# One-core sparse attention and mixture of experts: a new hand-written order of all steps, a rotated identity for the key turns, split loads of the first batch, merged weight loads, and a reciprocal written back to PSUM

## The chip, the cores and the metric

One Trainium2 chip, one of its cores, one launch. The time is device microseconds (us) of that core. The engines named below are TensorE (PE; PEld is its weight load), VectorE (DVE), ScalarE (ACT), GpSimd (POOL) and SyncE (SP, which here only issues transfers). POOL issues transfers too; they are called software transfers here, after the profile's name for their queue.

## The reference

Two stages on batch 4, 8 heads, 768 positions, head size 64. The first is a sparse attention: each query sees its neighbours nearer than 16 positions and 24 summaries (one for each block of 32 keys: the largest key value of each column, and the mean of the block's values). The second takes the result, 768 x 512 for each batch, through a router and four causal attention experts of head size 64, of which each position uses the best two.

```python
k_sum = k.reshape(B, H, nb, block, D).max(axis=3)      # nb = 24, block = 32
v_sum = v.reshape(B, H, nb, block, D).mean(axis=3)
scores_l_m = np.where(abs(i - j) < 16, scale * q @ k.T, -1e9)
scores_s = scale * q @ k_sum.T + log(block)
attn = softmax(concat(scores_l_m, scores_s)) @ concat(v, v_sum)
x = attn  # heads side by side: (B, 768, 512)
logits = x @ w_gate                                     # 4 experts, the best 2 with their weights w
for e in range(4):
    a = softmax(causal(scale * (x @ wq[e]) @ (x @ wk[e]).T))
    out += w_e * (a @ (x @ wv[e]) @ wo[e])
```

## The kernel before

The program is a plan of named steps, each a few instructions on one engine, and a table written out by hand (`TABLE`) that lists every step once, in one global order, with the engine that does it (P, V, A, G or S for PE, DVE, ACT, POOL, SP) and the buffer or PSUM bank that each new tile takes. Each engine runs its own steps strictly in the order of the table; waits between engines follow from who writes and reads which part of which tile. PSUM has eight banks and every tile class a fixed number of slots (`SLOTS`), so the table also fixes who waits for a slot.

Names are step, batch, then a number. For the first stage a batch has four pairs of heads (0 to 3), and two groups of two pairs, which share a load of keys and queries:

- Loads: `dk`, `dq` (keys, queries of a group, software transfers with a cast to 16 bits, issued by POOL), `dv` (values of a pair, four transfers from SP), `dvs` (values once more in the layout for block means, four transfers).
- `hc` copies the 32-row edges of the value tile `vb`, on POOL, ACT or DVE. Block means: `bs` (PE with the constant `sel`), `be` (DVE, four instructions) and `ds` (spreads the means into rows 96 to 119 of `vb`), or for the groups in `TREE` adds on POOL (`tr`, L340, the first of 1,024 columns and then 512 to 64) and `ds`.
- `tk`, `tq` (PE turns keys and queries, L359), `kw` (keys out of PSUM into windows), `rk` (block maximum, DVE), `ksc` (the maxima copied beside each window), `cq` (queries out of PSUM), `sc` (scores: the mask `mt` times `pi`, L407, then L413), `ex` (exponentials on ACT, L420), `av` (times `vb`, L430), `rc` and `xm` (normalising, DVE), `tx` (turn, L455), `hi`, `lo` (two 16-bit halves).
- Second stage, per batch: `vp` (values and router logits, L539 and L542), `lg`, `v2` (copies), `ga`, `gx`, `gb`, `gc` (router), and for two pairs of experts `pp`, `pc` (queries and keys, L607), six blocks of `sp`, `es`, `dm` (scores L631, exponentials L639, causal mask on POOL L644), `aw` (times values, L655), `r2` (reciprocal L674, times the router's weight L676), `wv` (L681), `tw`, `ct` (turn and copy), and per batch `op`, `oc`, `od` (output matmul L709, copy, store).

`r2` takes the column of sums (column 64 of each block) out of PSUM: L674 writes its reciprocal to the small SBUF tile `cmb`, and L676 multiplies `cmb` by the router's weight `gt`, both in SBUF, back into `cmb`.

The key tiles `kn` are 100 rows: two rows of zeros, 96 of keys, two of zeros. Setup fills each of the three whole (`knz`, L219, DVE), so a key load waits for that fill. The turn with the plain identity puts the zero columns at both ends of each 100.

A step `fill` exists that runs matmuls on zeros; the table before doesn't use it. The first instructions before are, on POOL, `dk001 dk000 dq001 id16 dq000 mt sel hc00`, where `id16`, `mt` and `sel` make constants.

Of the kernel before, what the change touches and what calls it, by code (L numbers as in the profile page):

```python
# [15 lines left out]
S = 768  # L16
# [44 lines left out]
227,P,3.1.0 246,V, 14,G, 53,P,6.0.0 54,A, 34,S,3 229,V, 96,P,0.1 97,A, 70,P,4.1.1 35,G, 36,P,2.1 55,V, 207,G,2
231,P,0.1 217,G,0 114,S,0 115,S, 216,G,0 71,A, 247,A, 37,V, 33,G, 38,V, 118,S, 84,P,6.0.2 72,V, 230,G, 83,P, 85,V,
232,A, 248,P,2.2 228,A, 86,V, 249,A, 100,P,0.1.0 101,P, 117,S, 102,V, 103,V, 235,P,4.3 250,P,2.2 87,P,6.2.2 236,A,
251,A, 88,V, 89,V, 252,P,4.4 122,G, 104,P,0.3.3 261,P,2.2.2 253,A, 105,A, 106,V, 278,P,3.0.0 280,V, 124,G, 265,P,4.0
282,P,5.2 262,A, 279,A, 283,A, 263,V, 281,V, 266,A, 210,S,4 208,S,5 209,G, 168,P,0.0 170,P,6.1 264,G, 233,P,2.5 234,A,
169,V, 211,G, 212,P,0.0 284,P,2.1 116,S,1 267,P,4.0 113,S, 171,V, 110,S, 119,S, 121,V, 129,P,6.0.0 285,A, 213,V,
215,A, 109,S, 112,S, 214,V, 268,A, 131,V, 130,A, 126,P,0 127,V, 132,P,2 134,A, 108,S, 111,S, 123,V, 222,S,0 128,V,
178,P,4.0 133,V, 135,V,0 175,P,6 176,A, 376,G,1 184,P,0 185,A, 223,G, 238,P,2.0.1 237,P, 239,V, 240,V, 255,P,6.1.2
179,A, 254,P, 256,V, 257,V, 136,A, 137,V, 224,G,0 180,G, 187,P,0 269,P,2.3 188,A, 189,G, 186,G, 241,P,4.4.4 242,V,
243,V, 218,S,0 120,S, 270,A, 172,P,0 173,A, 181,P,6 182,A, 139,P,2.2 140,A, 258,P,0.5.5 259,V, 260,V, 177,G, 183,G,  # L70
138,V, 141,P,6.0 174,G, 191,P,0.0.2 192,P, 219,A, 220,S,1 190,P, 193,V, 194,V, 286,P,0.5 221,V, 142,A, 158,P,4.0
225,G, 272,P,6.0.0 381,S,0 287,A, 159,A, 146,P,0 147,A, 152,P,4 153,A, 375,G,1 149,P,2 271,P, 273,V, 274,V, 150,A,
226,G, 288,P,0.1.1 289,P, 155,P,4 143,P,6 156,A, 386,G,2 275,P,2.6.6 290,V, 291,V, 144,A, 276,V, 277,V, 292,P,0.7.7
382,G, 293,A, 294,V, 195,P,4.0 125,A, 151,G, 401,P,5.1 196,A, 402,V, 383,G,1 397,P,6.1.1 160,G, 154,G, 399,V,
418,P,7.0 419,A, 339,P,2.1 340,A, 398,V, 337,P,0.0 148,G, 145,G, 162,P,1.1.4 161,P, 157,G, 163,P, 164,V, 165,V,
379,S,2 338,A, 356,P,0.1 341,P,2 385,V, 298,P,6.1.1 300,V, 299,V, 342,A, 357,A, 400,A, 344,P,4 384,G,3 380,G, 345,A,
353,P,2 354,A, 295,P,0 296,V, 297,V, 301,P,6 302,A, 350,P,0 351,A, 403,P,2.4 377,S, 358,G, 347,P,4 303,V, 414,P,6.2.0
551,S,0 304,V,1 416,V, 348,A, 404,A, 431,P,7.0.2 433,V, 390,S,5 308,P,0.2 309,A, 166,P,4.1 167,A, 310,P,2.0 311,A,
405,P,0.2 406,A, 417,V, 432,V, 305,A, 200,P,4.0 415,V, 546,G,2 312,P,2.0 327,P,6 328,A, 556,G,0 422,P,0.3 378,G,
387,G,0 346,G, 355,G, 420,P,6.0 201,V, 306,V, 307,V, 349,G, 313,A, 352,G, 421,A, 343,G, 360,P,0.0.4 423,A, 361,P,  # L80
359,P, 362,V, 363,V, 203,P,2.1 204,A, 435,P,6.2 436,V, 324,P,0 325,A, 545,G,1 315,P,4 316,A, 364,P,7.2 552,G, 553,G,0
365,V, 197,P,2.2 555,G,4 321,P,0 322,A, 448,P,6.1.1 329,G, 198,V, 450,V, 451,V, 318,P,4 434,G, 452,P,7.1 453,V,
425,P,2.0.2 319,A, 567,P,0.2.0 569,V, 424,P, 426,V, 427,V, 408,P,4.1.0 449,A, 456,P,6.1 391,G, 407,P, 409,V, 410,V,
568,A, 457,A, 570,V, 437,P,0.5 438,A, 392,S,0 454,P,2.3 455,A, 317,G, 571,P,6.0 588,P,7.1 584,P,0.1.2 585,A, 572,A,
205,S, 326,G, 557,G,1 589,V, 320,G, 323,G, 314,G, 586,V, 330,P,1.1.4 331,P, 332,P, 333,V, 334,V, 439,P,2.0 411,P,0.0.0
440,A, 393,G, 394,G,1 396,V, 388,S,0 573,P,6.2 574,A, 587,A, 395,G, 575,P,2.4 576,A, 412,V, 428,P,4.1.1 413,V, 389,G,
199,S, 458,P,6.1.1 459,P, 429,A, 590,P,2.3 442,P,0.0.2 460,V, 461,V, 591,A, 430,V, 441,P, 605,P,2.2 443,V, 444,V,
592,P,6.1 606,A, 335,P,3.3 462,P,4.2.2 463,V, 445,P,0.3.3 464,V, 336,A, 369,P,2.1 593,A, 446,A, 447,V, 562,S,0 563,G,
564,G,1 366,P,6.2 367,A, 507,P,4.1 509,P,0.0 508,V, 370,A, 202,S, 565,V,1 468,P,2.0.0 469,V, 510,A, 526,P,0.1 520,P,4
554,G,2 527,A, 528,G, 547,S, 470,V, 521,A, 522,G, 465,P,6 466,A, 467,V, 511,P,0 514,P,2 512,A, 622,P,4.0 623,V,  # L90
618,P,5.0.1 515,A, 620,V, 471,P,6 516,G, 523,P,0 473,A, 472,V, 517,P,2 621,G, 524,A, 601,P,4.2.0 518,A, 525,G, 619,V,
372,P,6.0 373,A, 603,V, 478,P,0.2 479,A, 602,V, 558,S, 474,V,0 480,P,2.0 481,V, 548,G, 578,P,4.1.0 475,A, 513,G,
577,P, 476,V, 477,V, 371,S, 497,P,0.0 498,A, 549,S, 604,G, 607,P,2.0 626,P,6.5 579,V, 580,V, 519,G, 529,P,0.0.0 368,S,
531,P, 608,A, 530,P, 627,A, 532,V, 533,V, 624,P,2.4 625,A, 491,P,6 492,A, 550,G, 595,P,4.0.1 374,S, 499,G, 594,P,
596,V, 597,V, 609,P,0.2 610,A, 485,P,2 581,P,6.4.4 582,V, 488,P,4 486,A, 566,G,3 583,V, 489,A, 559,G, 612,P,0.1.2
611,P, 560,S, 561,G, 613,V, 614,V, 598,P,2.5.5 599,A, 482,P,4 628,P,6.0.0 483,A, 629,P, 600,V, 494,P,0 630,V, 493,G,
487,G, 631,V, 495,A, 615,P,2.6.6 616,A, 617,V, 534,P,4.0 535,V, 632,P,6.7.7 490,G, 484,G, 496,G, 502,P,1.1.0 501,P,
500,P, 503,V, 504,V, 633,A, 648,P,2.1 649,A, 650,P,4.0 651,A, 634,V, 505,P,0.1 681,P,2.2 682,V, 661,P,4.1 658,P,6
506,A, 536,P,0.1 537,V, 638,P,2.1.1 640,V, 662,A, 659,A, 664,P,4 665,A, 667,P,6 639,A, 641,P,0 642,V, 668,A, 655,P,4
656,A, 666,G, 657,G, 652,P,2 653,A, 643,A, 683,P,6.0 538,S, 684,V, 635,P,4 636,V, 660,G, 669,G, 644,V,1 700,P,0.0  # L100
701,A, 663,G, 654,G, 688,P,2 689,A, 690,G, 637,V, 539,P,6.2 540,V, 541,S, 685,P,0 702,G, 671,P,0.0.4 645,A, 686,A,
670,P, 694,P,2 695,A, 672,P, 646,V, 647,V, 677,V, 678,V, 687,G, 696,G, 673,V, 691,P,0 697,P,6 674,V, 542,P,2.0 692,A,
693,G, 704,P,1.1.0 703,P, 706,V, 707,V, 698,A, 699,G, 675,P,4.2 543,A, 544,S, 705,P, 710,V, 711,V, 676,A, 679,P,2
680,A, 708,P,3.3 712,P,2 713,V, 720,P,2.1 709,V, 721,A, 722,S, 714,P,0.2 715,V, 716,S, 717,P,4.0 718,A, 723,P,0.1
719,S, 724,A, 725,S,
# [51 lines left out]
def make_plan(nc, T, q, k, v, moe_w_gate, moe_wq, moe_wk, moe_wv, moe_wo, out):  # L157
# [23 lines left out]
    vones, knzs = [st("vo0"), st("vo1")], [st("kz0"), st("kz1")]  # L181
# [24 lines left out]
    def vone(i0, i1):  # L206
        def go(e):
            for t in T["vb"][i0:i1]:
                en(e).memset(t[0:96, :, 64:65], 1.0 / XS)
                en(e).memset(t[96:128, :, 64:65], 32.0 / XS)  # L210
                en(e).memset(t[0:16, 0:24:12, :], 0.0)
                en(e).memset(t[64:96, 11:24:12, :], 0.0)  # L212
                en(e).memset(t[64:80, 11:24:12, 64:65], 1.0 / XS)
        return go

    def knz(i0, i1):
        def go(e):
            for t in T["kn"][i0:i1]:
                en(e).memset(t, 0.0)  # L219
        return go  # L220
# [27 lines left out]
    def load_qk(b, g, parts):  # L248
        n = 4 // parts
        kn[b, g], qn[b, g] = R.buf("kn"), R.buf("qn")  # L250
        for i in range(parts):
            h0 = 4 * g + n * i

            def gk(e, t=kn[b, g], i=i, h0=h0):
                nc.gpsimd.dma_start(
                    out=T["kn"][t.slot][PE0:PE0 + 96, n * i:n * i + n, :],
                    in_=k[b, h0:h0 + n].rearrange("h (p s) d -> p h (s d)", s=8))

            def gq(e, t=qn[b, g], i=i, h0=h0):
                nc.gpsimd.dma_start(  # L260
                    out=T["qn"][t.slot][:, n * i:n * i + n, :],
                    in_=q[b, h0:h0 + n].rearrange("h (p s) d -> p h (s d)", s=QT))
            R.step(f"dk{b}{g}{i}", {"G": 0.72}, knzs[0:1] if (b, g) == (0, 0) else knzs, [kn[b, g]], gk, dma=n * 96 * 0.098 / 16)
            R.step(f"dq{b}{g}{i}", {"G": 0.72}, [], [qn[b, g]], gq, dma=n * 128 * 0.077 / 16)

    vb, vr = {}, {}
# [594 lines left out]
```

## Time and profile before

| | us |
|---|---|
| median of 3 runs | 185.4 |
| the three runs | 181.22, 185.4, 187.53 |
| the profiled execution | 181.54 |
| its span, first to last instruction | 179.6 |
| outside the span (the difference) | 1.94 |

The profile is one execution. Busy time of an engine is the sum of its instructions; the slices cut the span into 40 parts of 4.49 us and show the busy share of each in tenths. The chain of work is followed back from the last instruction, at each step to what released it. An idle time is given in brackets with what ended it. In section 6 of the page the last number is the time from a transfer's issue to its landing. The chain has 50% of the span on PE, 30% on DVE, 7% on "issue", 4% each on ACT and transfers and 2% on POOL.

### The profile page before, as it was taken

The numbers are of one execution on the slowest core, as the hardware profiler recorded it, in microseconds if no ns is written. First come the engines' busy times: TensorE is split into PE (matmuls) and PEld (weight loads), VectorE is DVE, ScalarE is ACT, GpSimd is POOL, SyncE is SP. The second block draws the span as 40 slices with busy tenths as digits, with TensorE's granted clock in tenths as the row PEclk, the third lists the DMA queues.
The fourth block names the chain that finished last, engine by engine and source line by source line (L and its number), as shares of the span: only waits on it lengthen the run. The fifth ranks groups of instructions, "written<-read, shape, count | busy, mean of one in ns | idle before, by whom it ended". The sixth has DMA issues, their size and how long they took to land.

```text
span 179.6 us, 6545 instructions
## 1 busy us (share of the span) xinstructions
PE 147.4 (82%) x2784; PEld 110.7 (62%) x2784; DVE 135.9 (76%) x265; ACT 120.1 (67%) x155; POOL 99.3 (55%) x150
## 2 busy tenths in 40 slices
PE   0247569899999999979969959899988899999660
PEld 0235558677679778657546858766757787565420
DVE  5763875999796989897998929866999878538640
ACT  2056667947688978876987837476947674789640
POOL 5866353440993599987986990861377520053100
PEclk9999999999999999999999969999999999999996
DMA  4999999989985996499939959806461000032326
GB/s 72 167 217 229 217 161 192 213 166 169 220 143 122 151 168 96 113 145 200 161 84 217 251 128 210 178 4 184 141 169 39 7 0 4 0 120 105 127 98 257
DMA packets 44221, 25.34 MB, mean 141 GB/s; under 512 B 33216, under 2 KB 40384, under 8 KB 43712
## 3 DMA queue, kind: packets, MB, share of 16 engines
q1 hardware_dynamic: 36736, 18.63, 47.5%
q0 software_dynamic: 7456, 6.29, 23.6%
q8 instruction: 22, 0.36, 0.8%
q14 instruction: 7, 0.06, 0.1%
HBM read 24.91 MB, written 6.29 MB: 174 GB/s over the span
## 4 chain that ended last, share of the span: by engine, by line
PE 50%; DVE 30%; issue 7%; ACT 4%; DMA 4%; POOL 2%; DVEq 0%; ACTq 0%; POOLq 0%
PE ps L430 10%; PE ps L607 7%; PE ps L455 5%; PE ps L359 4%; PE ps L539 4%; PE ps L709 4%; DMA qn<-in_q_dram 4%; DVE vb L168 3%; PE ps L655 3%; DVE ks L375 3%; PE ps L631 3%; PE ps L407 3%; PE ps L297 3%; DVE wav L681 3%; DVE cmb L676 2%
## 5 line engine op out<-in xcount | busy, mean ns | idle before, releaser
L639 ACT ACTIVATE a<-ps 128x1024 f16<-128x1024 f32 (+1 forms) x48 | 41.9, 916 | 9.8 <-PE ps L631 8.8
L644 POOL TENSOR_SCALAR_AFFINE_SELECT a<-a 128x256 f16<-128x256 f16 x48 | 18.7, 408 | 37.7 <-ACT a L639 26.7
L420 ACT ACTIVATE aT<-ps 120x768 f32<-120x768 f32 x32 | 25.3, 817 | 10.0 <-PE ps L413 7.5
L340 POOL TENSOR_TENSOR vt<-vt 120x1024 f32<-120x1024 f32 (+3 forms) x20 | 25.1, 1254 | 5.7 <-DMA vt<-in_v_dram 4.5
L430 PE MATMUL ps<-vb,aT 120*64 120x65 f32 x768 | 26.3, 224 | 1.5 <-POOL wgt L510 0.5
L430 PEld LDWEIGHTS ps<-vb,aT 120*64 120x64 f32 x768 | 24.0, 138 | 3.9 <-issue 1.6
L607 PE MATMUL ps<-hi,wqk 128*128 128x384 f16 x128 | 22.6, 326 | 0.4 <-DVE lo L466 0.4
L166 ACT COPY kw<-ps 128x1152 f16<-128x1152 f16 x10 | 11.2, 1120 | 15.3 <-PE ps L359 10.2
L168 POOL COPY vb<-vb 32x1408 f32<-32x1408 f32 x13 | 18.1, 1398 | 2.0 <-DMA vb<-in_v_dram 1.4
L631 PE MATMUL ps<-qk,qk 64*128 64x512 f16 (+3 forms) x128 | 14.9, 307 | 4.2 <-DVE wav L681 2.9
L607 PEld LDWEIGHTS <-wqk 128*128 128x128 f16 x128 | 12.0, 98 | 8.6 <-issue 1.0
L375 DVE TENSOR_REDUCE ks<-ps 128x24 f16<-128x768 f16 x16 | 14.8, 948 | 2.0 <-ACT kw L166 2.0
L359 PE MATMUL ps<-id,kn 100*64 100x100 f16 x256 | 9.1, 223 | 8.8 <-POOL sel L236 7.7
L466 DVE TENSOR_TENSOR lo<-ps,hi 128x768 f16<-128x768 f32 x16 | 15.1, 954 | 1.6 <-ACT hi L166 1.2
L445 DVE TENSOR_TENSOR x<-ps,rec 128x768 f32<-128x768 f32 x16 | 15.3, 958 | 0.6
L539 PE MATMUL ps<-wvg,hi 128*128 128x264 f16 x96 | 13.9, 275 | 0.2 <-DVE lgp L168 0.2
L359 PEld LDWEIGHTS <-kn 100*64 100x64 f16 x256 | 7.5, 120 | 10.3 <-DVE vb L212 7.6
L455 PE MATMUL ps<-id,x 128*128 128x128 f32 x96 | 13.7, 280 | 0.1
L359 PE MATMUL ps<-id,qn 128*64 128x128 f16 x192 | 8.6, 234 | 6.2 <-DMA qn<-in_q_dram 2.2
L655 PE MATMUL ps<-v,a 128*128 128x65 f16 x336 | 12.8, 198 | 0.6 <-ACT wT L166 0.6
L655 PEld LDWEIGHTS <-a 128*128 128x128 f16 x336 | 12.1, 101 | 2.1 <-issue 1.4
L709 PE MATMUL ps<-wo,wT 128*128 128x512 f16 x48 | 12.0, 380 | 0.9 <-DVE wT L168 0.5
(94 smaller groups left out, 281.4 us busy)
## 6 DMA issues: line engine op xcount, KB each, us to landing
vb<-in_v_dram SPq DMA_DIRECT2D x32, 176.0 KB
out_dram<-ob SPq DMA_DIRECT2D x11, 512.0 KB
vt<-in_v_dram SPq DMA_DIRECT2D x20, 192.0 KB
kn<-in_k_dram POOLq DMA_DIRECT2D x7, 384.0 KB, 5.7
qn<-in_q_dram POOLq DMA_DIRECT2D x7, 384.0 KB, 6.9
a<-in_moe_wq_dram SPq DMA_DIRECT2D x4, 128.0 KB
a<-in_moe_wk_dram SPq DMA_DIRECT2D x4, 128.0 KB
a<-in_moe_wv_dram SPq DMA_DIRECT2D x4, 128.0 KB
```

The lines of the kernel that those rows point to most:

```text
L168: en(e).tensor_copy(dst, src)
L340: en(e).tensor_tensor(y[0:120], x[0:120, 0:w], x[0:120, w:2 * w], AL.add)
L359: nc.tensor.transpose(dst[64 * hp:64 * hp + 64, p * s:p * s + p], src[:, hh + hp, 64 * s:64 * s + 64], T["id16"][0:p, 0:p])
L375: nc.vector.tensor_reduce(T["ks"][ks.slot], view(pbank16(kp), PE0, [[4, NSUM], [KP, 8], [1, 4]]), AX.XY, AL.max)
L420: nc.scalar.activation(T["aT"][aT.slot][0:KR], pbank(sc, 2)[0:KR, :, 0:384], AF.Exp, scale=SCALE)
L430: nc.tensor.matmul(pbank(av, 2)[o:o + 64, u, 65 * (2 * (t // 2) + hp):65 * (2 * (t // 2) + hp) + 65], a[0:KR, hp, 64 * t:64 * t + 64], T[" ...
L455: nc.tensor.transpose(pbank(xp, 2)[:, t // 3, 128 * (t % 3):128 * (t % 3) + 128], T["x32"][x32.slot][:, 128 * t:128 * t + 128], T["id32"])
L539: nc.tensor.matmul(p[:, i, 0:264], hi_(ch)[:, cols], T["wvg"][:, ch, :], start=(ch == 0), stop=False, skip_group_check=True)
L607: nc.tensor.matmul(pbank(pp, 2)[:, u, 0:384], T["wqk"][:, cc, ch, j, :], hi_(ch)[:, 384 * u:384 * u + 384], start=(ch == 0), stop=(ch == N ...
L631: nc.tensor.matmul(pbank(sp, 2)[:, ep, c0:c0 + w], T["qk"][qk[1].slot][r, 128 * tj:128 * tj + 128], T["qk"][qk[0].slot][r, n0:n0 + w], sta ...
L639: nc.scalar.activation(a2v(u), pbank(sp, 2)[:, :, 0:ln], AF.Exp, scale=SCALE / (XS * XS))
L655: nc.tensor.matmul(pbank(av, 2)[:, ep, 65 * ti:65 * ti + 65], a2v(u)[:, ep, o:o + 128], T["v2"][v2.slot][:, tj, 2 * cc + ep, :], start=(tj ...
```

## The change

The table is another one: every step keeps its arithmetic, but the order on every engine, the engine of some steps, and slots and banks differ. Beside it:

```diff
-            for t in T["vb"][i0:i1]:            # vone: two steps, two and four tiles
+            t = T["vb"][bf.slot]                # vone: a step for each of the six tiles
...
-            for t in T["kn"][i0:i1]:
-                en(e).memset(t, 0.0)
+        for t in T["kn"]:
+            en(e).memset(t[96:100].bitcast(FP32), 0.0)
...
+        for j, r, n in ((0, 96, 2), (2, 0, 96), (98, 98, 2)):
+            en(e).tensor_copy(T["idr"][:, j:j + n], T["id16"][0:KP, r:r + n])
...
-                    out=T["kn"][t.slot][PE0:PE0 + 96, n * i:n * i + n, :],
+                    out=T["kn"][t.slot][0:96, n * i:n * i + n, :],
...
-            turn(pbank16(kp), T["kn"][kn[b, g].slot], 8, KP)
+            turn(pbank16(kp), T["kn"][kn[b, g].slot], 8, KP, T["idr"])
...
-        for ex_ in range(E):                    # one load for each expert of wq, wk, wv: 12
+        for cc in range(2):                     # one for each two experts: 6
...
-                    nc.vector.reciprocal(t, avv()[:, :, i0:i1, 64:65])
+                    t, d = T["cmb"][cm.slot][:, :, i0:i1, :], avv()[:, :, i0:i1, 64:65]
+                    nc.vector.reciprocal(d, d)
...
-                    nc.vector.tensor_tensor(t, t, g, AL.mult)
+                    nc.vector.tensor_tensor(t, d, g, AL.mult)
...
+    for i in range(12):                         # fl0 to fl11: two matmuls on zeros if on PE, nothing if on ACT
+        fb = R.buf("ps")
...
-                load_qk(b, g, 1)
+                load_qk(b, g, 2 if b == 0 else 1)
```

So the key rows now lie at rows 0 to 95 with four zero rows behind, only those four rows are filled, and the identity `idr`, whose columns are rotated by two, puts the zero columns where they were. Keys and queries of the first batch's second group come in two halves each, as the first group's did. The weight copies (`cvg`, `cw`) take the experts apart on the way into the 16-bit tiles; `cw` becomes two instructions. Of the twelve `fl` steps ten stand on ACT and issue nothing; `fl9` and `fl0` stand on PE behind the last output matmul.

How the head stands on three engines, up to the third `tx` (numbers are batch, pair, and the half of a score):

```
PE before:   tk01 tk00 tq00 tq01 sc001 sc000 bs00 tk03 tk02 sc011 sc010 tq02 tq03 av001 bs01 av000 bs02 sc021 sc020
             av010 av011 sc031 tk11 tk10 tx00 sc030 tx01 bs03 tq10 av021 av020 tq11 av030 av031 sc101 sc110 tx02
PE after:    tk01 tk00 tq01 tq00 bs00 sc010 tk03 bs01 sc011 tq03 sc000 tk02 sc001 av011 av010 av000 tk11 av001 tq02
             bs02 sc021 sc020 tx01 tk10 sc031 tq11 tq10 av020 bs03 sc030 sc110 av021 sc100 tx00 av030 av031 tx02
POOL before: dk001 dk000 dq001 id16 dq000 mt sel hc00 dk010 v2o dq010 hc01 vtz dk100 ksc03 id32 hc03 dq100 dq110 dk110
             ds02 ksc10 cg cw1 hc10
POOL after:  dk001 dk000 kwz id16 idr dq001 dk011 dq000 vtz dk010 dq011 id32 dq010 mt ksc00 sel hc01 dk100 ds01 dq100
             ksc02 cw1 dq110 ds02 hc03 dk110 ksc11 cg ksc10 ds03
ACT before:  kw00 ksc01 cq00 kw01 cq01 ex001 ex000 kw02 ex010 cq02 cq03 ex011 ksc02 ds01 ex021 ex020 ex031
ACT after:   hc00 kw00 ksc01 cq01 kw01 ex010 cq00 ds00 cq03 ex011 ex000 ksc03 kw03 ex001 kw02 cq02 kw11 ex021 ex031
```

Steps that change engine, as counts before and after: DVE `v2` 9 to 4, `cq` 5 to 3, `kw` 6 to 5, `ksc` 5 to 3, `ds` 6 to 4, `hc` 2 to 4, `ct` 4 to 8; ACT takes `v2` 3 to 8, `cq` 11 to 13, `kw` 10 to 11, `hc` 1 to 2, and gives `ct` 6 to 2. In the third quarter POOL's order before has all six `dm10` masks of batch 1 ahead of `tr210` and `tr211`; after, it runs `ds30 dm115 dk300 tr210 dm104 dm101 dq310 ksc23 ksc22 dk310 dm103 tr211 dm105 dm102 dm100`. The last outputs before are `op32 op30 op31 op33` with `op33` in the bank that `op30` had; after, `op33` has a bank of its own.

More of the change, by code (lines that the diff above doesn't have):

```diff
@@ L61 @@
[L61 to L65, printed above, removed]
@@ L365, in tk @@
         def tk(e):
[L366 to L367 removed]
+            turn(pbank16(kp), T["kn"][kn[b, g].slot], 8, KP, T["idr"])
+        R.step(f"tk{b}{c}", {"P": 0.38}, [kn[b, g], idr, knzs], [kp], tk, mode=2, keep=[kw, ks])
         def kwc(e):
@@ L793 @@
     one("id16", (128, 128), HALF)
+    one("idr", (KP, KP), HALF)
     one("id32", (128, 128), FP32)
```

181 lines of the change are left out of this document (95 added, 86 removed).

## Prediction

> **What bounds the kernel now.** The page first: busy times and the slices.
>
> ```profile
> span 179.6 us, 6545 instructions
> PE 147.4 (82%) x2784; PEld 110.7 (62%) x2784; DVE 135.9 (76%) x265; ACT 120.1 (67%) x155; POOL 99.3 (55%) x150
> PE   0247569899999999979969959899988899999660
> ```
>
> PE is busiest and idle for 179.6 - 147.4 = 32.2 us. The slices put that idle time at the two ends. The view by stages counts it:
>
> ```profile
> 0.00:42.50 42.50, 27.01 (x682) 22.41 (x684) 30.27 (x79) 24.19 (x31) 22.08 (x42) 1.00 1.06 183
> 42.50:103.00 60.50, 56.09 (x1072) 41.90 (x1066) 53.52 (x92) 48.15 (x62) 48.34 (x63) 1.00 0.92 158
> 103.00:109.00 6.00, 3.82 (x79) 3.50 (x78) 2.69 (x5) 2.40 (x3) 4.79 (x7) 0.72 0.60 153
> 109.00:160.00 51.00, 48.60 (x815) 36.09 (x816) 39.36 (x61) 35.05 (x47) 20.20 (x29) 1.00 0.35 88
> 160.00:180.00 20.00, 11.84 (x149) 6.84 (x147) 10.10 (x30) 10.28 (x15) 3.90 (x11) 0.91 0.36 132
> ```
>
> The columns are length, then busy time of PE, PEld, DVE, ACT and POOL, the granted clock, transfers. PE idles 15.5 us of the first 42.5, 4.4 and 2.4 in the two long middle stages, 2.2 in the six about 103, 8.2 in the tail. No step of PE's arithmetic is removed, so a gain must come out of these.
>
> **The head.** The third `tx` ends at 39.30 + 0.87 = 40.2. Both orders put the same PE steps ahead of it, so I ask when the new order gets there.
>
> ```profile
> 2.31 1.45 POOL L255 DMA_DIRECT2D kn<-in_k_dram  x2 [1.79 <-DVE vb L209]
> 7.97 0.19 POOL L238 TENSOR_SCALAR_AFFINE_SELECT sel<-sel 96x2 f32<-96x2 f32 x1
> 11.67 1.49 PE L359 MATMUL ps<-id,qn 128*64 128x128 f16 x24 [2.20 <-DMA qn<-in_q_dram]
> 14.81 1.40 PE L297 MATMUL ps<-vb,sel 96*32 96x128 f32 x24
> 22.44 0.87 PE L297 MATMUL ps<-vb,sel 96*32 96x128 f32 x24
> 39.30 0.87 PE L455 MATMUL ps<-id,x 128*128 128x128 f32 x6
> L255 POOL DMA_DIRECT2D kn<-in_k_dram x9: 645/687/1354, 2.3 to 85.4; - x9
> L260 POOL DMA_DIRECT2D qn<-in_q_dram x9: 721/756/1090, 3.7 to 96.7; - x9
> L244 POOL MEMSET vt<- x1: 1795/1795/1795, 13.7 to 13.7; 128x2048 f32 x1
> L228 POOL MEMSET v<- x2: 224/253/282, 10.2 to 10.3; 128x24 f16 x2
> ```
>
> Key loads waited for the DVE fills until 2.31; with only rows 96 to 99 filled they needn't, and POOL can begin at about 0.8, when the others do. That is not free, for `mt` and `sel` are moved behind it all. Before, POOL did two key halves, two query halves, `id16`, `mt` and `sel` from 2.31 to 8.16: 5.85 us. The new queue adds two key halves (2 x 0.69), two query halves (2 x 0.76), `vt` (1.80) and nine small fills and copies (three for `kw`, three for `idr`, two for `id32`, one `ksc`; about 0.28 each from L228): 7.2 us. So `sel` is ready at 0.8 + 5.85 + 7.2 = 13.9. The first block sums, at 14.81 before, then start at 13.9 to 14.9 with handovers; I take 14.1, ending at 15.5 at the same slow 1.40.
>
> The gain is behind that: the second sums (22.44 before, behind query turns that waited for ACT) stand two steps after the first. From there ACT carries the chain:
>
> ```profile
> L420 ACT ACTIVATE aT<-ps 120x768 f32<-120x768 f32 x32 | 25.3, 817 | 10.0 <-PE ps L413 7.5
> L166 ACT COPY kw<-ps 128x1152 f16<-128x1152 f16 x10 | 11.2, 1120 | 15.3 <-PE ps L359 10.2
> L166 ACT COPY qT<-ps 128x768 f16<-128x768 f16 x11 | 8.6, 804 | 3.4 <-PE ps L359 3.4
> L168 POOL COPY vb<-vb 32x1408 f32<-32x1408 f32 x13 | 18.1, 1398 | 2.0 <-DMA vb<-in_v_dram 1.4
> L168 POOL COPY vb<-vs 24x1536 f32<-24x1536 f32 x1 | 1.5, 1462 | 3.3 <-DVE vs L315 3.3
> L315 DVE TENSOR_TENSOR vs<-ps,vs 24x128 f32<-24x128 f32 x14 | 4.1, 292 | 0.5
> L430 PE MATMUL ps<-vb,aT 120*64 120x65 f32 x768 | 26.3, 224 | 1.5 <-POOL wgt L510 0.5
> ```
>
> Score of `sc010` at 15.5, done 16.15; ACT then runs four `ex` (3.3), two `cq` (1.6), one `kw` (1.1), `ds00` (1.46) and `ksc` (0.4) without a gap, to 24.0. PE: `av001` (26.3 / 32 steps = 0.8), `tq02` (1.49 for two, about 0.4 each at full clock), `bs02` 0.87, to 26.2; DVE's four instructions of `be02`, each like L315, 1.2 to 1.3, POOL's `ds02` and `hc03` 2.9, to 30.4; `av020` and `bs03` 1.6, `be03` 1.3, `ds03` 1.5, `av030` and `av031` 1.6, `tx` 0.9: 37.3. That is 2.9 us ahead of 40.2, but some twenty handovers at 0.05 stand in no row of mine. I take **2.0 us gained**. Ends: 2.9, and, if the eight issues took L255's and L260's longest (1.354, 1.090), 4 x 0.67 + 4 x 0.33 = 4.0 us later, a loss of 2.0. What is early in the order has slack until then. A query half landed at 11.67 before and costs nothing up to `sel`'s 13.9; the four-row fills that are left to DVE delay only the key turns ahead of that. On ACT the table load and `hc00` now stand behind the first value load, and with two `kw`, `ksc` and `cq` they are due by 15.5: 1.4 + 2.2 + 0.4 + 0.8 = 4.8 us, so nothing is lost unless the values land after about 9.
>
> The added half loads don't pay by themselves:
>
> ```profile
> kn<-in_k_dram POOLq DMA_DIRECT2D x7, 384.0 KB, 5.7
> kn<-in_k_dram POOLq DMA_DIRECT2D x2, 192.0 KB, 5.3
> ```
>
> A half landed 0.4 us sooner than a whole one, for one more issue of 0.69, already in the sum. The Trainium skill, "DMA: Bandwidth & Descriptors", Anatomy of one DMA, gives a software transfer a fixed 2.0 us and then its bytes at 436 GB/s: an estimate by it is 2.9 us for a whole load and 2.5 for a half, so it too makes the difference 0.4 us, and both landings here are over twice its figure. Six weight loads in place of twelve save six issues on SP, which is on no chain: nothing; if SP's were, their 0.4 us each.
>
> **The reciprocal.** This is the edit with the clearest price.
>
> ```profile
> L676 DVE TENSOR_TENSOR cmb<-cmb,gt 128x12 f32<-128x12 f32 x6 | 3.8, 637 | 0.2
> L676 DVE TENSOR_TENSOR cmb<-cmb,gt 128x8 f32<-128x8 f32 x2 | 0.3, 174 | 0.1
> L681 DVE TENSOR_TENSOR wav<-ps,cmb 128x768 f16<-128x768 f32 x6 | 5.7, 958 | 0.2
> 76.22 1.35 POOL L168 COPY vb<-vb 32x1408 f32<-32x1408 f32 x1
> 76.47 1.13 DVE L676 TENSOR_TENSOR cmb<-cmb,gt 128x12 f32<-128x12 f32 x1
> PE ps L631 <- DVE wav L681: 2.9, 3, 1.7
> ```
>
> Twelve columns take 637 ns in the mean, eight take 174. The last rows show why: the multiply that began at 76.47 ended at 77.60, with POOL's copy (77.57). It reads two SBUF tiles; L681, with one PSUM operand, is never stretched. After the change L676 has a PSUM operand, so 6 x (0.637 - 0.18) = 2.75 us of DVE goes, on the way to `wav`, for which PE waited 2.9 us. I take **2.0 us gained**: the next late thing will keep some. Ends: 2.75, and nothing (the new order might have parted the two engines anyway). The write into PSUM has no row; were each of the ten pairs slower by a whole multiply of 0.18, 1.8 would be lost, which I give little weight.
>
> **The rest.** Steps that change engine: DVE sheds five `v2`, two `cq`, one `kw`, two `ds`, and takes two `hc` and four `ct`, a few us in all, which ACT takes. In the middle PE's idle time is only 4.4 + 2.4, so this may bring or cost up to 3 us; I take 0. The tail:
>
> ```profile
> 173.80 0.59 PE L709 MATMUL ps<-wo,wT 128*128 128x512 f16 x2 [0.45 <-DVE ob L168]
> ```
>
> The last output waited 0.45 for a bank; it has its own now: **0.4 gained**. The four added zero matmuls stand behind it, under 5.2 us of copy and store to 179.6: nothing.
>
> Sum: 2.0 + 2.0 + 0.4 = 4.4. The profiled execution was 181.54 (the span and 1.94 outside it), so its like would take 177.1. It is at the low end of runs whose median is 185.4, 2.1% above it; the same for the changed kernel would be 180.9, and between the two I say **179.0**.
>
> **Rivals.** *The gains are eaten*: in the new order the next operand is as late as the old one, since DVE was 53.5 of 60.5 us busy in the long stage and still feeds everything. For it: 88% there. Against: the head's idle time isn't DVE's. Time: 181.5 by the profile, 185 by the median.
>
> *Tree sums block the masks* (slower). `tr210` now stands ahead of the six masks of its half batch, two key-sum copies and two loads in POOL's order; before, it stood behind them.
>
> ```profile
> 112.69 5.06 POOL L340 TENSOR_TENSOR vt<-vt 120x1024 f32<-120x1024 f32 x4 [4.50 <-DMA vt<-in_v_dram]
> L340 POOL TENSOR_TENSOR vt<-vt 120x1024 f32<-120x1024 f32 x5 | 11.8, 2362 | 4.6 <-DMA vt<-in_v_dram 4.5
> 104.00:105.00 1.00, 0.00 (x0) 0.00 (x0) 0.00 (x0) 0.00 (x0) 0.84 (x3) 0.85 0.07 18
> 105.00:106.00 1.00, 0.79 (x18) 0.79 (x20) 0.25 (x1) 0.00 (x0) 0.90 (x3) 0.50 0.00 0
> 107.00:108.00 1.00, 1.00 (x23) 1.00 (x21) 0.38 (x1) 1.00 (x2) 1.00 (x1) 0.50 0.97 219
> PE ps L359 <- issue: 2.2, 1, 2.2
> ```
>
> A tree waited 4.5 us for its transfer, then its first add takes 2.36: 6.9 us. If PE runs dry that long its clock falls: after the gap of 2.2 us the clock stood at 0.50 for some three us, 1.7 us of work lost. The Trainium skill, "TensorE: Matmul & The Clock Gate", Part 1, has the clock fall to half after an idle window of about 3.4 us; by that a gap of 2.2 need not do it, but this trace shows that it did. Price 6.9 + 1.7 - 4.4 = 4.2: 185.7 by the profile (2.3% slower), 189.6 by the median. It decides from where PE has no other steps for the 6.9 us; against it, some ten matmul steps stand between.
>
> *The head doesn't move*, because first loads land as before: 177.1 + 2.0, 179.1 to 183.
>
> **Numbers.** Within 2%, about what runs of this kernel can tell from no change, lies 177.9 to 185.2 in the profile's terms and 181.7 to 189.1 in the median's. Forecast (177.1 or 180.9): 0.48, faster. Eaten gains: 0.20, and the unmoved head: 0.10, both the same. Blocked masks, or another step that POOL's order holds up as long: 0.22, slower. The forecast's own range goes from 172 (2.9 + 2.75 + 0.4 and 3 from the middle leave 172.5) to 182; to hold 8 in 10 it reaches up through the middle cases and into the slow one, to 189.
>
> **What will show it.** L676 at 0.18 throughout; the second sums near 17 in place of 22.4; the third `tx` near 38; `sel` done near 14; POOL not idle ahead of `tr210`. I am wrong if PE's idle time before 42 stays at 15, or if a gap of over 2 us opens in the middle.

## The result, and the profile after

The changed kernel takes 175.3 us (median of four runs, 172.95 to 178.16), the kernel before 183.7 beside it (181.22 to 187.53): a ratio of 0.955, 95% interval 0.940 to 0.970, faster. Ratios, here and below, are taken over each kernel's fast runs alone (those within 1.5% of its fastest), and by that rule the profiled execution of the changed kernel, 176.72 us, is a slow one and that of before, 181.54, a fast one. Medians take all runs. Of the 176.72 us the span has 175.0. From the page after, the span, the busy times and TensorE's slices:

```profile
span 175.0 us, 6544 instructions
PE 149.3 (85%) x2788; PEld 110.8 (63%) x2788; DVE 131.6 (75%) x252; ACT 122.5 (70%) x162; POOL 102.1 (58%) x163
PE   0439998789999986999995999989999999999770
```

PE is busy 1.9 us longer, the zero matmuls among it, in a span that is 4.6 shorter: the gain is idle time (32.2 us before, 25.7 after). Where it went is seen by cutting both spans at the ends of the same five TensorE steps: the third `tx` (`tx02`), `av200`, `tx22`, `tx33`, and the last output `op33`. The view by stages, of before and then of after (length; busy PE, PEld, DVE, ACT, POOL; granted clock; transfers):

```profile
0.00:40.18 40.18, 24.69 (x616) 20.38 (x618) 28.15 (x76) 22.00 (x28) 22.08 (x42) 1.00 1.07 181
40.18:101.47 61.29, 56.91 (x1084) 42.70 (x1085) 54.27 (x91) 48.81 (x63) 46.89 (x62) 1.00 0.92 156
101.47:118.19 16.72, 13.92 (x320) 12.19 (x320) 11.72 (x18) 10.16 (x14) 11.39 (x13) 0.90 0.77 172
118.19:148.52 30.33, 28.52 (x495) 21.14 (x493) 25.20 (x42) 20.96 (x28) 14.30 (x22) 1.00 0.29 80
148.52:174.39 25.87, 23.32 (x280) 14.33 (x276) 16.61 (x40) 17.50 (x24) 4.66 (x12) 1.00 0.20 73
```

```profile
0.00:40.09 40.09, 27.16 (x616) 21.46 (x618) 27.23 (x66) 22.24 (x26) 27.84 (x53) 1.00 1.11 190
40.09:102.80 62.71, 57.18 (x1079) 42.32 (x1080) 54.67 (x88) 49.61 (x70) 45.99 (x63) 1.00 0.84 142
102.80:115.15 12.35, 12.35 (x313) 10.79 (x312) 11.60 (x20) 10.42 (x14) 7.39 (x12) 1.00 1.07 201
115.15:145.15 30.00, 29.49 (x525) 21.86 (x525) 22.30 (x40) 22.50 (x30) 16.19 (x25) 1.00 0.30 87
145.15:168.84 23.69, 22.20 (x266) 14.14 (x262) 14.54 (x41) 17.12 (x22) 4.74 (x12) 1.00 0.28 101
```

The orders put slightly different steps between two cuts, so the counts of matmuls differ by a few. The head gives 0.1 us, the long stretch takes 1.4 *more*, the third gives 4.4 (PE idle 2.8 before, nothing after, and the clock from 0.90 to 1.00), the fourth 0.3, the fifth 2.2. From `op33`'s end to the span's is 6.2 in place of 5.2. That is the 4.6, and most of it lies where the prediction's sum had no term. TensorE's busy time in the first row rose from 24.69 to 27.16 us for the same 616 matmuls, since more of them ran at the slow rate (the second block sums took 1.51 us where they took 0.87), and that ate up what the head lost of idle time.

Three places of the timeline explain the stretches. First the head (start, duration, what ran, idle time before it and its releaser):

```profile
13.51 1.51 PE L302 MATMUL ps<-vb,sel 96*32 96x128 f32 x24 [0.37 <-POOL sel L242]
16.50 1.51 PE L302 MATMUL ps<-vb,sel 96*32 96x128 f32 x24
33.36 0.64 PE L302 MATMUL ps<-vb,sel 96*32 96x128 f32 x14 [1.19 <-issue]
```

The block sums start where they were put, at 13.5 and 16.5. Then TensorE stops for 1.19 us between the tenth and the eleventh matmul of one step (`bs03`), waiting for nothing that the profile shows. In this execution that is why the third `tx` is not early.

Second, DVE. The groups of some of its small instructions (busy us, mean ns | idle before):

```profile
L588 DVE SCALAR_TENSOR_TENSOR gt<-gt 128x24 f32<-128x24 f32 x4 | 3.0, 741 | 0.1
L598 DVE TENSOR_TENSOR gt<-gt 128x24 f32<-128x24 f32 x4 | 2.8, 692 | 0.1
L681 DVE RECIPROCAL ps<-ps 128x12 f32<-128x12 f32 x6 | 1.4, 234 | 0.6 <-PE ps L662 0.6
L683 DVE TENSOR_TENSOR cmb<-ps,gt 128x12 f32<-128x12 f32 x6 | 1.0, 171 | 0.2
```

L683 is the multiply of the reciprocal: 171 ns where it was 637. But two groups of the router's instructions on `gt`, with two SBUF operands each, now average 0.7 us. One instruction of each did it, in the timeline:

```profile
61.89 5.03 POOL L345 TENSOR_TENSOR vt<-vt 120x1024 f32<-120x1024 f32 x4
61.99 2.29 DVE L588 SCALAR_TENSOR_TENSOR gt<-gt 128x24 f32<-128x24 f32 x1
...
92.62 2.34 POOL L345 TENSOR_TENSOR vt<-vt 120x1024 f32<-120x1024 f32 x1 [0.64 <-DMA vt<-in_v_dram]
92.79 2.22 DVE L598 TENSOR_TENSOR gt<-gt 128x24 f32<-128x24 f32 x1
...
96.41 0.39 PE L638 MATMUL ps<-qk,qk 64*128 64x512 f16 x2 [2.32 <-DVE wav L688]
```

An instruction of some 0.2 us that begins beside POOL's tree addition ends with it. The second time TensorE pays 2.32 us, through `wav` behind it. The Trainium skill, "SBUF — State Buffer", Who interferes with whom, says that a DVE instruction with two SBUF inputs contends with a GpSimd instruction that reads SBUF, since the second input comes through a read interface that the two share, and that the lock on it is exclusive; these rows agree (2.29 and 2.22 us).

Third, the tail:

```profile
168.96 1.23 DVE L168 COPY ob<-ps 128x1024 f32<-128x1024 f32 x1 [2.29 <-DMA out_dram<-ob]
169.57 0.58 ACT L166 COPY ob<-ps 128x512 f32<-128x512 f32 x1 [0.85 <-DMA out_dram<-ob]
```

`op33` waited for no bank, but the last two output copies waited for the stores of earlier outputs to free their tiles.

### The profile page after: what moved, and what is told of

Its sections match the earlier page's. It is cut to its first block, busy times and chain, and to the rows that moved or that the text cites. A ratio compares the mean times of both kernels' runs of the same rounds, so it can differ in the third digit from the quotient of the medians.

```text
span 175.0 us, 6544 instructions
## 1 busy us (share of the span) xinstructions
PE 149.3 (85%) x2788; PEld 110.8 (63%) x2788; DVE 131.6 (75%) x252; ACT 122.5 (70%) x162; POOL 102.1 (58%) x163
## 4 chain that ended last, share of the span: by engine, by line
PE 49%; ACT 15%; DVE 12%; POOL 9%; issue 9%; DMA 3%; POOLq 0%; ACTq 0%; DVEq 0%
PE ps L435 10%; PE ps L614 7%; ACT a L646 5%; PE ps L546 5%; PE ps L460 4%; PE ps L364 4%; PE ps L638 4%; ACT aT L425 3%; PE ps L662 3%; DMA out_dram<-ob 3%; PE ps L716 3%; ACT kw L166 3%; PE ps L412 3%; PE ps L302 2%; DVE vb L168 2%
## 5 line engine op out<-in xcount | busy, mean ns | idle before, releaser
L651 POOL TENSOR_SCALAR_AFFINE_SELECT a<-a 128x256 f16<-128x256 f16 x48 | 19.3, 421 | 38.3 <-ACT a L646 37.9
L345 POOL TENSOR_TENSOR vt<-vt 120x1024 f32<-120x1024 f32 (+3 forms) x20 | 24.5, 1226 | 4.0 <-DMA vt<-in_v_dram 2.9
L168 POOL COPY vb<-vb 32x1408 f32<-32x1408 f32 x10 | 13.4, 1349 | 5.0 <-DMA vb<-in_v_dram 4.5
L364 PE MATMUL ps<-idr,kn 100*64 100x100 f16 x256 | 9.7, 224 | 6.7 <-DMA kn<-in_k_dram 6.7
L166 ACT COPY kw<-ps 128x1152 f16<-128x1152 f16 x11 | 12.3, 1125 | 2.2 <-DVE ks L380 1.8
L662 PE MATMUL ps<-v,a 128*128 128x65 f16 x336 | 12.1, 193 | 1.4 <-DVE lo L471 1.3
L662 PEld LDWEIGHTS <-a 128*128 128x128 f16 x336 | 11.3, 97 | 3.0 <-issue 1.8
L168 POOL COPY vb<-vu 24x768 f32<-24x768 f32 x14 | 12.2, 875 | 0.7
```

Of the source, the lines that this page charges most:

```text
L168: en(e).tensor_copy(dst, src)
L345: en(e).tensor_tensor(y[0:120], x[0:120, 0:w], x[0:120, w:2 * w], AL.add)
L364: nc.tensor.transpose(dst[64 * hp:64 * hp + 64, p * s:p * s + p], src[:, hh + hp, 64 * s:64 * s + 64], idt)
L651: nc.gpsimd.affine_select(m, m, [[0, 2], [1, 128]], AL.is_ge, 0.0, base=0, channel_multiplier=-1)
L662: nc.tensor.matmul(pbank(av, 2)[:, ep, 65 * ti:65 * ti + 65], a2v(u)[:, ep, o:o + 128], T["v2"][v2.slot][:, tj, 2 * cc + ep, :], start=(tj ...
```

## The experiments

Eleven kernels ran; each time is the median of six runs, with the ratio to the kernel before beside it on the same chip (its median 183.3, 183.3 and 184.0 in the three groups).

| kernel | us | ratio, 95% |
|---|---|---|
| changed kernel again | 176.6 | 0.958, 0.945 to 0.970 |
| before + reciprocal in PSUM | 182.5 | 0.987, 0.977 to 0.996 |
| changed, reciprocal in SBUF | 180.6 | 0.980, 0.971 to 0.989 |
| all edits, order of before | 186.8 | 1.021, 1.013 to 1.029 |
| the same, rotated identity on POOL | 184.7 | 1.013, 1.003 to 1.022 |
| before, stream shifted by 64 matmuls | 186.5 | 1.027, 1.014 to 1.040 |
| changed, `gb0` and `tr210` moved | 176.8 | 0.976, 0.965 to 0.986 |
| changed, six output tiles | 174.7 | 0.963, 0.953 to 0.972 |
| changed, whole loads | 176.9 | 0.970, 0.956 to 0.983 |
| changed, `dk110` earlier | 174.7 | 0.958, 0.950 to 0.967 |
| changed, `dk110`, `gb0`, six output tiles | 172.7 | 0.947, 0.938 to 0.955 |

**The changed kernel again.**

> The changed kernel once more, for its spread and for a second profile. All theories: a median of 175 us (172 to 178), 0.94 to 0.97 of the kernel before. Theory 'the order' and theory 'the edits' say nothing different here. Theory 'the stall' (the kernel before stands still for 2.2 us near 103 us and then runs at half clock, because matmul instructions come late, and the changed kernel doesn't): again no idle stretch of all engines of over 1 us between 95 and 115 us, the third tx again near 40 to 41 us. If holding by the tree sums is in the order, the last multiply of the router (L598) takes about 2.2 us once again, near 93 us, beside the first addition of tr210; if it is chance of one execution, 0.18.

176.6 us. The profile (173.93 us) ends its five cuts at 38.82, 100.55, 112.90, 142.41 and 166.10: the stretch of 12.35 comes out the same to the hundredth, the head doesn't. No stop in `bs03`, none at 95 to 115. This execution's span is 7.4 us shorter than before's, nearer to the difference of the medians (8.4 in the result, 6.7 here): 1.4 in the head, 0.4 longer in the long stretch, then 4.4, 0.8 and 2.2, and 0.9 longer behind `op33`. The hold by `tr210` is chance:

```profile
92.57 0.18 DVE L598 TENSOR_TENSOR gt<-gt 128x24 f32<-128x24 f32 x1
92.86 2.35 POOL L345 TENSOR_TENSOR vt<-vt 120x1024 f32<-120x1024 f32 x1 [1.09 <-DMA vt<-in_v_dram]
```

The multiply was through 0.1 us before the addition began, since POOL had waited longer for its transfer. L588, beside `tr200`, was held as before (a mean of 740 ns).

**The reciprocal, alone in the order of before.**

```diff
-                    nc.vector.reciprocal(t, avv()[:, :, i0:i1, 64:65])
+                    t, d = T["cmb"][cm.slot][:, :, i0:i1, :], avv()[:, :, i0:i1, 64:65]
+                    nc.vector.reciprocal(d, d)
```

> The kernel before with one edit alone: the reciprocal's result stays in PSUM and the multiply reads it from there; order and all else as before. My prediction: 2.0 us faster than the kernel before (2.75 at most, 0 at least), about 181.5 us; the twelve-column multiplies fall from 637 to about 180 ns. Theory 'the order' (the new order makes all the gain): within 0.5 us of the kernel before, 183 to 184. Theory 'the edits': at least half of the 8 us, 180 or less. Theory 'the stall': its profile shows the idle stretch of some 2 us near 103 us with the clock at 0.50 behind it again, since it has the order of the kernel before; if that was chance, no such stretch.

The ratio of 0.987 is 2.5 us, with an interval of 0.7 to 4.3; the medians of all runs differ by 0.8 alone. In its profile the stretch from `tx02` to `av200` takes 59.5 us (45.03 to 104.54) against 61.3 before: 1.8 gained where the multiplies stand. The stop of the kernel before, two rows of this run, and its multiplies:

```profile
105.21 0.43 PE L359 MATMUL ps<-id,qn 128*64 128x128 f16 x4 [2.18 <-issue]
```

```profile
107.73 0.30 PE L359 MATMUL ps<-id,qn 128*64 128x128 f16 x4 [1.63 <-issue]
119.15 0.40 PE L691 MATMUL ps<-id,wav 128*128 128x128 f16 x4 [1.27 <-issue]
```

```profile
L676 DVE TENSOR_TENSOR cmb<-ps,gt 128x12 f32<-128x12 f32 x6 | 1.0, 171 | 0.2
```

The stop, at 103 us before, is here too, in the same step, between the same two matmuls of the query turn `tq31`. It belongs to the order. A wait for the step's operands it can't be, since eight of its twelve matmuls had run.

**The reciprocal, undone in the new order.**

```diff
-                    nc.vector.reciprocal(d, d)
-                    nc.vector.tensor_tensor(t, d, g, AL.mult)
+                    nc.vector.reciprocal(t, d)
+                    nc.vector.tensor_tensor(t, t, g, AL.mult)
```

> The changed kernel with one edit undone: the reciprocal goes to SBUF again and the multiply reads two SBUF tiles; order and all else as in the changed kernel. My prediction's term: 2.0 us slower than the changed kernel, about 177.3 us (between 175.3 and 178.1). Theory 'the order': within 0.5 us of it, since the multiplies that are held now stand where others wait for nothing. The profile: the twelve-column multiplies of this line go from 171 ns to 180 where POOL does nothing beside them and to 1 us or more where it does; I expect a mean of 300 to 650 over the six.

180.6 us, 4.0 slower by the medians, and the two intervals don't overlap (0.945 to 0.970, 0.971 to 0.989). The profile shows less at the line itself:

```profile
L683 DVE TENSOR_TENSOR cmb<-cmb,gt 128x12 f32<-128x12 f32 x6 | 2.2, 371 | 0.2
```

```profile
41.68 0.88 PE L364 MATMUL ps<-idr,kn 100*64 100x100 f16 x16 [2.83 <-DMA kn<-in_k_dram]
95.41 2.35 POOL L345 TENSOR_TENSOR vt<-vt 120x1024 f32<-120x1024 f32 x1 [0.72 <-DMA vt<-in_v_dram]
95.65 2.15 DVE L595 TENSOR_TENSOR gt<-gt 128x24 f32<-128x24 f32 x1
```

Six multiplies at 371 in place of 171 are 1.2 us. The other two rows are things that happen to the changed order too: a key load that came 2.83 us late, and the hold by `tr210`, this time of L595. So the edit's price in the new order is 1.2 us at its line (one multiply of 1.32 us beside a tree addition holds TensorE for 0.73 until 84.07) and 4.0 by the times; what makes up the difference stays open.

**All edits in the order of before.** The table is the old one, with the new steps set into it; the four zero matmuls are left out.

> All edits of the change (rotated identity and four-row fills, half loads, six weight loads, reciprocal in PSUM), but the steps in the order and on the engines of the kernel before, the zero matmuls left out. Theory 'the order': 182 to 185, no faster than the kernel before with the reciprocal edit alone. Theory 'the edits': 175 to 178. Between them by my prediction's sum: reciprocal minus 2.0, smaller fills let the first key load go out earlier, up to minus 1.5 at the head if values and masks follow, so 180 to 182. Theory 'the stall': an idle stretch of about 2 us near 100 to 103 us with a fall of the clock again.

> As the run with all edits in the order of the kernel before (186.8 us), but the rotated identity is made on POOL right behind the identity instead of on DVE, where TensorE's first turn waited for it until 10.2 us. If that place was what made it slow: 183 to 184, still no gain, since the added half loads and the rotated identity stand ahead of the selection matrix on POOL. If the added half loads are: 186 to 187 again. The stall ahead of tq31 stays in both.

186.8 and 184.7 us: the edits alone make nothing faster. The waits of TensorE and the timeline of the first, then of the second:

```profile
PE ps L364 <- DVE idr L223: 10.2, 1, 10.2
110.31 0.30 PE L364 MATMUL ps<-id,qn 128*64 128x128 f16 x3 [1.54 <-issue]
```

```profile
PE ps L364 <- POOL mt L193: 5.7, 1, 5.7
106.63 0.30 PE L364 MATMUL ps<-id,qn 128*64 128x128 f16 x3 [1.29 <-issue]
```

With the rotated identity on POOL the first key turn starts at 5.7 in place of 7.7, yet the first block sums end at 17.7, 1.5 later than before (16.2): ahead of them the query turns wait for their loads until 10.7 and the scores `sc001` and `sc000` another 1.8 us for `pi`, which DVE makes. The new order puts the block sums ahead of those scores, and so can use the earlier keys. And the stop in `tq31` is there in all four profiles of the old order: 2.18, 1.63, 1.54, 1.29 us.

**Shifting the instruction stream.** Counted from the first, the stops of all profiles fall between the same numbers of TensorE's matmuls: 474 and 475 (`bs03` after), 600 to 602, 1746 to 1748 (`tq31`), 2000 to 2002. They lie about 127 apart, or a multiple of it, which with the weight loads is about 254 instructions, and the list of transfer queues (packets, MB, share) of before has one of their size:

```profile
q8 instruction: 22, 0.36, 0.8%
```

That is 22 blocks of 16384 bytes; TensorE's 2784 matmuls and as many weight loads make 253 instructions for each. So I put 64 matmuls ahead of all; the fill of their zeros, `zz`, moves to right behind `knz0` on DVE.

```diff
-            nc.tensor.matmul(T["ps"][:, bank, :], T["zz"][:, 0:128], T["zz"], start=True, stop=True)
+            nc.tensor.matmul(T["ps"][:, bank, 0:64], T["zz"][:, 0:128], T["zz"][:, 0:64], start=True, stop=True)
```

> The kernel before with 64 small matmuls of zeros (128x64) into a bank that nothing uses yet, put ahead of the first key turn, where TensorE waits until 7.7 us anyway. They leave the order of all else as it is and only push every later TensorE instruction 128 places down in the instruction stream. In the three profiles of the order of the kernel before, TensorE stands still ahead of the same step each time (the query turn tq31: 2.2, 1.6 and 1.5 us) and restarts 1.3 to 1.7 us after a transfer of 16384 bytes of TensorE instructions has ended. Theory 'instruction transfers' : the place of the stall follows the position in the stream, so the stall ahead of tq31 goes or shrinks under 0.5 us, stalls may stand elsewhere, and the time falls by the part that is not made up again: 179 to 182 if no other falls in a bad place, 183 if one does. Theory 'something that tq31 itself waits for' (its query load, its bank): the stall ahead of tq31 stays at 1.5 to 2.2 us and the time at 183 to 184.

```profile
33.79 0.77 PE L455 MATMUL ps<-id,x 128*128 128x128 f32 x5 [1.56 <-issue]
48.63 0.30 PE L359 MATMUL ps<-id,kn 100*64 100x100 f16 x2 [3.00 <-issue]
109.39 0.69 PE L430 MATMUL ps<-vb,aT 120*64 120x65 f32 x16 [0.91 <-issue]
110.78 0.86 PE L359 MATMUL ps<-id,qn 128*64 128x128 f16 x24
```

`tq30` and `tq31` (the last row, 24 matmuls) now run through in 0.86 us, and the stop stands in `av200`, 16 matmuls from its end: those 16, two scores of 14 and 20 of the 24 are 64. It moved by exactly what was put in, so it hangs on the position in the stream and not on the step. My price for it was wrong in sign: 186.5 us, slower. One stop shrank from 2.2 to 0.9, and two at other marks (1.56 and 3.00, matmuls 475 and 728) took its place, each with the clock at 0.50 for 3.4 us behind it.

Why it stops at one mark and not at the next is in the transfer records. Mark 1619 is the last before `tq31`'s; the block's transfer starts some time after TensorE has passed it, and in every stop that I measured TensorE went on 1.3 to 1.9 us after a transfer had ended:

```
kernel                          matmuls 1619 to 1746 take   transfer starts    transfer   stop at 1746
before                          4.0 us                      4.1 us after 1619  0.96 us    2.18 us
before + reciprocal             4.0                         3.4                0.93       1.63
all edits, order of before      4.0                         3.6                0.94       1.54
the same, identity on POOL      4.0                         3.3                0.93       1.29
before, shifted                 4.1                         2.6                1.15       0.91
changed                         4.7                         2.3                0.97       none
changed, again                  4.7                         1.6                1.01       none
```

Start, transfer and some 1.5 us: 6.6 us in the first row, 2.6 more than the block lasts; 4.8 in the row of the changed kernel, where it lasts 4.7. In the old order the 127 matmuls behind mark 1619 are all of turns, scores and `av`, some 0.03 us each; in the new one six of a `tx` are among them (0.88 us for the six), so the block lasts 0.7 longer, and the transfer starts 1 to 2 us sooner. The start goes with the load on the transfers: in the 4 us about mark 1619 the transfer share of the view by stages (its last column but one: the transfers' time over that of the 16 engines that carry them) is 1.03 to 1.12 in the five profiles of the old order and 0.78 to 0.92 in the eight of the new one. Over the marks of all 13 profiles the transfer began 0.1 us after its mark in the median where that share was under 0.2 (45 marks), and 1.9 us where it was 0.9 or more (92). No run changed that load alone. The Trainium skill, "Runtime: NRT & Kernel Launch", Instruction fetch mechanics, tells of these blocks and calls their cost mostly hidden; here it was not, by up to 3.0 us at a time.

**The two moves for the router.** `gb0` goes to just before `gc0` on DVE, `tr210` to just before `tr211` on POOL.

> The changed kernel with two steps moved in the order: the router's gb0 on DVE to just before gc0, so that its two-SBUF instructions don't stand beside the tree additions of tr200; the first tree addition tr210 on POOL to just before tr211, away from the router's gb1 and gc1. Theory 'held DVE instructions cost time in the new order': L588 and L590 and all other router instructions at 0.18 to 0.4 us in every execution, DVE 3 us less busy; 1 to 2 us faster than the changed kernel, 174.6 to 175.6 against its 176.6, since the 2.2 us at L598 fell on TensorE in one profile of two. Rival: the move makes tr211 and the value sums of the fourth group late by the 2.4 us of the addition, the av2x steps wait, and the time is the same or up to 2 us longer.

```profile
L588 DVE SCALAR_TENSOR_TENSOR gt<-gt 128x24 f32<-128x24 f32 x4 | 0.9, 227 | 0.1
L598 DVE TENSOR_TENSOR gt<-gt 128x24 f32<-128x24 f32 x4 | 0.7, 184 | 0.1
```

The holds are gone, the time is no better (176.8; ratio 0.976 beside 0.958 of the changed kernel again). Against the profile of the changed kernel again, the steps from `sp002` to `sp003` took 3.8 us in place of 5.2, and those from `tq32` to `sc300` 5.6 in place of 4.9; what was left by the end was lost and won elsewhere, so here the rival held, in part.

**Six output tiles.** `ob` 3 to 6, the last four outputs in tiles of their own.

> The changed kernel with six output tiles instead of three, so that the last four output copies don't wait for earlier stores. Before this, the last copy on DVE waited 2.29 us for a store (1 us of it after its matmuls were done) and the last on ACT 0.85. Theory 'the tail waits for output tiles': 0.7 us faster than the changed kernel, 175.9 against 176.6, and no wait for a store in the last 8 us. Rival: the stores are serial at the end anyway, so the last one only starts earlier and lands at the same time: same within 0.3.

174.7 us, but no gain by the ratio (0.963 beside 0.958 of the changed kernel again): no copy waits for a store any more, and yet `op33`'s end to the span's end is 6.0 us in place of 6.1. The stores are last one way or the other. The other 1.7 us between the medians lie within what these runs scatter.

**Whole loads.** The first batch's second key and query group in one load each.

> The changed kernel with the first batch's second key group and second query group in one whole load each instead of two halves (two issues fewer on POOL). My prediction said that the added halves don't pay by themselves: two issues of 0.69 and 0.76 stand ahead of the selection matrix, so sel is done about 1.4 us earlier (12.0 instead of 13.45), the first block sums start up to 1.4 us earlier, at 12.1 to 13.5, and the time is 0 to 1.4 us shorter than the changed kernel, 175.2 to 176.6. Rival: the half loads let the key turns tk03 and tq03 come early; with whole loads these wait and the head is up to 1 us longer, 177.6.

```profile
13.55 0.85 PE L364 MATMUL ps<-id,qn 128*64 128x128 f16 x12 [2.78 <-DMA qn<-in_q_dram]
14.33 1.51 PE L302 MATMUL ps<-vb,sel 96*32 96x128 f32 x24
...
44.27 0.88 PE L364 MATMUL ps<-idr,kn 100*64 100x100 f16 x16 [3.33 <-DMA kn<-in_k_dram]
```

`sel` is done at 12.2, 1.3 earlier, as reckoned. It buys nothing, because `tq00`, ahead of the block sums on PE, now waits until 13.55 for its queries, and the block sums start 0.8 later than with halves. 176.9 us: same. The last row is the wait of the reciprocal's run again, in a kernel that differs in nothing near it: `dk110`, issued at 31 to 32 us, comes at its own time, 5.3 to 12.0 us later in six profiles.

**That key load earlier.** `dk110` moves on POOL ahead of `ds02`, whose operand POOL stands waiting for.

> The changed kernel with one load moved: the first key load of batch 1's second group (dk110) on POOL ahead of ds02, whose operand POOL waits 3.4 us for, so that it is issued near 25 us in place of 31.3. In four of six profiles of this order TensorE waited for that load at 40.6 to 44.3 us, 1.3 to 3.3 us, and then ran the turn at a lower clock. Theory 'late key load': that wait goes in the profile, tk13 ends near 39.7 to 40.5 instead of 41.0 to 45.2, and the median falls by 1 to 2 us, to 174.6 to 175.6 (against 176.6 and 176.8 of the changed order before). Rival: transfers are saturated between 20 and 40 us (DMA share 1.1), so the key load only changes places with the value loads; the av and bs steps wait for values instead and the time is the same within 0.5.

> The changed kernel with three things together: dk110 earlier as in the run just described, gb0 just before gc0 on DVE (tr210 left where it is), and six output tiles. If the single effects add up: minus 1 to 2 for the key load, minus 1.4 for gb0 (the stretch from sp002 to sp003 took 3.8 us with it in place of 5.2), minus 0.7 to 1.5 for the output tiles: 172.2 to 174 us. If the next late operand keeps each gain: 175 to 176.5.

174.7 us for the load alone, but its ratio is that of the changed kernel again (0.958), so no gain is shown. The load is issued at 24.55, `tk13` has no wait and ends at 39.1 (41.0 and 41.1 in the two profiles of the changed kernel). The profile met the hold by `tr210` again (`wav`, 2.5 us). With `gb0` and the output tiles, 172.7 us, a ratio of 0.947, the lowest here, though its interval overlaps the changed kernel's. The page of this last kernel:

```profile
span 171.1 us, 6541 instructions
PE 149.5 (87%) x2788; PEld 111.3 (65%) x2788; DVE 127.5 (75%) x252; ACT 122.3 (71%) x162; POOL 103.2 (60%) x163
PE   0438999799998999899999999989999999999680
```

Against before's slices, the dip to 5 at 103 to 108 us is gone and the second to fourth slices are fuller (438 for 247).

## Why the prediction was right or wrong

The range and the likeliest case held: 175.3 us, in 172 to 189, faster by 4.5% with an interval that leaves out 2%; the single number, 179.0, was 3.7 too high. The sum behind it came to 4.4, near the profiled difference of 4.8, but by other terms: that the two agree is luck.

*The head* (2.0 at the third `tx`). The walk was right as far as it went: `sel` at 13.45, first sums at 13.51 (I said 14.1), second at 16.50 (17). The third `tx` ended at 40.09 in the profile on record, not near 38; with the same head it ended at 38.82, 38.41 and 38.36 in three other profiles, where TensorE did not stop in `bs03`, and at 41.11 in one where it stopped 1.98 us in `av031`. So the term held when the instruction stream let it, and stood in no row that I had. The other mistake was to measure against one profile: the same old head, in the run with the reciprocal alone, reached the third `tx` at 45.03 in place of 40.18. Most of that is the rate of the matmuls. The same 616 kept TensorE busy for 24.69 us in before and for 28.66 there (28.99 and 28.56 with all edits in the old order, 26.7 to 27.5 in the new one); the same query turns, before and then with the reciprocal alone:

```profile
20.88 0.86 PE L359 MATMUL ps<-id,qn 128*64 128x128 f16 x24 [1.86 <-ACT kw L166]
22.68 1.49 PE L359 MATMUL ps<-id,qn 128*64 128x128 f16 x24 [0.91 <-ACT kw L166]
```

They ran fast from 16 us on in before and from 27 there. So before's profile has an uncommonly early head, and may hide a gain of the new one; what sets that moment no run shows. PE's idle time before 42 us, my sign, fell from 15.5 to 12.9.

*The half loads* ("don't pay by themselves") are worth 0.8 us at the first block sums, since a landing of half the bytes lets `tq00` go; in the time no difference is shown. A reading of mine was off there: the whole load's 5.7 us is just under twice the 2.9 of the estimate, only the half's 5.3 is over twice its 2.5.

*The reciprocal* (2.0): its line fell to 171 ns, and the time by 2.5 (0.7 to 4.3, by the ratio) in the old order. The write into PSUM cost nothing (234 ns for 228). What the sum left out is that the hold follows whoever stands beside POOL: it went to the router's instructions, some 2 us each time. That these two holds are why the stretch from 40 to 101 is 1.4 longer and not 2 shorter is argued from the rows; in the profile again, with one of them and a key load 1.34 us late, it is 0.4 longer, and with both moved away the steps behind the first took 1.4 less.

*The tail* (0.4): the wait for the bank is gone, but from `op33`'s end to the span's it takes 1.0 more than before, and without the waits for output tiles still 0.8 more. The zero matmuls end at 169.71, under the stores.

*The rest* (0, give or take 3) is the step that failed. It brought 4.4 in the stretch behind 101 us, the same again in the second profile, and 2.5 after it (3.0 there). I had the stop of 2.18 us and the half clock behind it quoted, under a rival, and counted it as a price for PE running dry, not as a loss that another order could drop. With the clock it is most of the 4.4: 2.18 of idle time, and 1.57 less busy time, a little of it seven fewer matmuls. In the fifth stretch PE's idle time falls from 2.55 to 1.49, by waits of 0.4 to 0.6 for `wav`, `wT` and `ob`; the remainder is other steps between the cuts. That the edits alone don't make this, the two kernels with all of them in the old order show (1.021 and 1.013); the new order without the edits was run for the reciprocal alone (0.980).

*The blocked masks*: `tr210` waited 0.6 to 1.6 us for its transfer in the seven profiles that have it in its new place, not 4.5, and TensorE was not held through the masks (its longest wait for any operand behind 50 us is the 2.32). The sign to watch for, a gap of over 2 us in the middle, did open (2.32 at 96.41), by the hold on DVE; the clock stayed at 1.00 behind it, so the 1.7 us that I had priced for its fall were not lost there. In those seven profiles it came three times.

## What to carry to other kernels

A wait of no visible cause that falls in the middle of a step, at the same matmul in each profile, was here the instruction stream: count the matmuls, and shift them to see whether the stop keeps its place. Where quick small ones fill a whole block while the transfers are full, slower ones among them might help; here they came together with a lighter load, so that advice is not tested by itself. When an operand is moved to PSUM to take one instruction out of POOL's way, look at every other two-SBUF instruction that the new order puts beside POOL. And take two or three profiles of the kernel before: the rate of the first matmuls, landings and stops moved its head by 5 us with not one instruction of the head changed.

## What the runs showed of the hardware

TensorE's instructions come in blocks of about 254 here, and passing one cost up to 3.0 us; the stop kept its place in the stream when 64 matmuls were put ahead. The block's transfer began later where the transfers were full (1.9 us after the mark in the median, against 0.1).

The clock stood at 0.50 for 3.4 us about the stop of 2.18 us in the kernel before, and for as long behind the stop of 1.56 us in the shifted kernel. It stood at 1.00 after stops of 1.27 to 1.63 in the run with the reciprocal alone, and after the wait of 2.32 in the changed kernel. So the length of a stop alone does not decide it.

Key loads took 5.7 us from issue to landing in the median of the kernel before; one of them, `dk110`, took from 5.3 to 12.0 when issued at 31 to 32 us.
